# A fused linear-attention and feed-forward kernel: the sums of weights all on VectorE, and a new order, new banks and other zero products

## The chip, the cores and the metric

The kernel runs on one core of a Trainium2 chip. The metric is the device time of one execution in microseconds (us), as the median of several runs. A core has TensorE for matrix products (PE in the profile; PEld is its loading of weights), VectorE (DVE), ScalarE (ACT), GpSimd (POOL) and SyncE (SP), which here issues the DMA transfers. Each engine takes its instructions from a queue of its own, in order; an instruction that waits holds up all behind it on its engine.

## The reference

```
B, H, S, D = 4, 8, 768, 48          # attention; then 3072 tokens x 384
for t in range(S):
    cur = einsum('bhd,bhe->bhde', u[None] * k[:, :, t], v[:, :, t])
    y[:, :, t] = einsum('bhd,bhde->bhe', r[:, :, t], state + cur)
    state = w[:, :, t, :, None] * state + einsum('bhd,bhe->bhde', k[:, :, t], v[:, :, t])
x = y as (3072, 384)
h = x @ w_in                        # 384 -> 2048
g = where(h >= 1, h, where(h <= -1, 0, (h + 1) ** 2 / 4))
out = g @ w_out                     # 2048 -> 384
```

## The kernel before

The attention is cut into 12 units of 256 tokens, each into four chunks of 64, in which the recurrence is products of matrices: VectorE makes running products of the decays w (scans, L461 and L466) and scales r and k with them (L484); TensorE makes the products inside a chunk (L518), transposes (L588) and products with the state (L657, L622); VectorE keeps the part of the L518 products that belongs to earlier tokens (a predicated copy, L531).

The feed-forward part runs over 6 blocks of 512 tokens and 16 tiles of 128 ff columns. Every operand is split into a high and a low part, and a product is the sum of three. The 16 weight tiles are unpacked once: ScalarE L356 and L361, VectorE L375 and L378, ScalarE L352 for the high part, VectorE L382 for the low part. In blocks 0 to 2 a tile is a product with w_in (L1334, nine matmuls 128x512 into one PSUM bank), the gate on ScalarE and VectorE (L1113 to L1127) and a product with w_out (L1354, nine matmuls).

Blocks 3 to 5 use a scheme after Strassen for the product with w_out (`fast`). It works on pairs of ff tiles. The product with w_in is as before (L1334), then come ScalarE's Relu and Square (L939, L940) and VectorE's L941, which reads the bank for the last time and so frees it. VectorE makes differences of gates (L961, L963, L965), each is split by ScalarE (L946, L956) and VectorE (L947, L957), and TensorE accumulates terms of three matmuls 128x256 (L979) into six banks. That leaves two of the eight PSUM banks for the L1334 products.

The scheme also needs sums of weights, made once for each of the eight pairs by `sums_of`: two sums 128x256 and four or five 128x128 in one scratch area (`a` and `s`, parts of the tile p), ScalarE's copy of the high part (L915), and the low part, a subtraction 128x512. A pair can begin only when the pair before it is through with the scratch. Even pairs are computed by VectorE, odd ones by GpSimd; ScalarE's copies are the same for both.

Twelve loads of w through one buffer (`last`), each followed by ScalarE's L794 and L795, guard against decays for which the scheme of the chunks doesn't hold. The next of these loads can start only when ScalarE is through with the one before. They stand between ScalarE's steps for blocks 2 and 3.

A plan collects the 1,780 operations of all this, and three tables written out as numbers decide where they go: `ORDER` is the order in which they are emitted, and so the order of each engine's queue; `BANKS` gives each of 186 tenants of PSUM its bank; `FILLS` puts products with zeros (`zeros`, L307, results never read) ahead of given operations, which keep TensorE busy where it would stand still. Each entry of `FILLS` is (operation, bank, columns, added to what is there or not). The costs given to the plan's operations play no part in what is emitted.

Of the kernel before, what the change touches and what calls it, by code (L numbers as in the profile page):

```python
# [222 lines left out]
def attention_moe(tc, a):  # L223
# [667 lines left out]
    def sums_of(pair):  # L891
# [21 lines left out]
        for x, to in parts:  # L913
            n = to.stop - to.start
# [503 lines left out]
```

## Time and profile before

| what | us |
|---|---|
| median of three runs | 493.82 |
| the runs | 493.41 to 495.09 |
| the profiled execution | 493.96 |
| its span, first to last instruction | 492.4 |
| TensorE busy in it | 476.5 |
| VectorE busy | 405.9 |
| ScalarE busy | 308.4 |
| GpSimd busy | 27.9 |

The span is that of one profiled execution; what lies outside it is 1.56 us. A share of busy time is a mean over the whole span. The rows further down show single stretches of it: how long each engine was busy in a stretch, when an instruction started, how long it took, and behind it in brackets how long its engine had stood still and what ended that.

### The profile page before, as it was taken

Reading aid. Unit: us, or ns where it says so; the run is one execution under the profiler, and the core shown is the slowest. Engines: PE = TensorE matmul, PEld = TensorE weight load, DVE = VectorE, ACT = ScalarE, POOL = GpSimd, SP = SyncE. Lnnn points to the kernel's source line nnn. Section 1 sums busy time; section 2 is a strip of 40 time slices with the busy share of each in tenths; the row PEclk is TensorE's granted clock in tenths of the full one; section 3 lists DMA queues with packets and bytes.
Section 4 is the critical chain, followed back from the end, with each engine's and each line's share of the span. In section 5 each row is a group of like instructions: output and inputs, shape, how many; then the busy total and the mean of one; then the engine's idle time right before and its main releaser. Section 6 shows DMA issues by size and latency. Waiting matters only on the chain.

```text
span 492.4 us, 13209 instructions
## 1 busy us (share of the span) xinstructions
PE 476.5 (97%) x5629; PEld 414.9 (84%) x5629; DVE 405.9 (82%) x627; ACT 308.4 (63%) x581; POOL 27.9 (6%) x49
## 2 busy tenths in 40 slices
PE   6899999999999999999999998999999999999994
PEld 3679988889999988888888787887988998899894
DVE  5999999999998998998978875885868576784673
ACT  3869999736446564666535748887668365473660
POOL 4000000000000000000000331432000000000000
PEclk9999999999999999999999999999999999999999
DMA  8959923126460634634441013323110000010002
GB/s 306 368 189 398 379 85 110 62 74 203 139 208 4 229 94 139 208 125 137 125 147 48 29 31 87 64 54 76 23 64 2 0 1 1 29 37 0 1 3 70
DMA packets 35203, 53.50 MB, mean 109 GB/s; under 512 B 15744, under 2 KB 22592, under 8 KB 35136
## 3 DMA queue, kind: packets, MB, share of 16 engines
q1 hardware_dynamic: 34992, 52.45, 32.0%
q8 instruction: 46, 0.75, 0.6%
q14 instruction: 21, 0.17, 0.1%
q10 hardware_dynamic: 144, 0.13, 0.1%
HBM read 46.86 MB, written 4.72 MB: 105 GB/s over the span
## 4 chain that ended last, share of the span: by engine, by line
PE 83%; DMA 8%; ACT 4%; issue 2%; DVE 1%; SPq 1%; ACTq 0%
PE ps L1334 35%; PE ps L1354 19%; PE ps L979 15%; DMA last<-in_w 6%; PE ps L657 4%; PE ps L518 3%; PE ps L588 2%; PE ps L622 2%; PE ps L307 1%; ACT last L795 1%; ACT last L794 1%; PE ps L1218 1%; DMA wraw<-in_wbits 1%; DMA cst<-in_consts 1%; SPq L777 1%
## 5 line engine op out<-in xcount | busy, mean ns | idle before, releaser
L1334 PE MATMUL ps<-x,wt 128*128 128x512 f32 (+1 forms) x972 | 208.0, 366 | 2.0 <-DVE rk L941 1.6
L1334 PEld LDWEIGHTS ps<-x,wt 128*128 128x128 f32 x972 | 162.9, 188 | 30.2 <-DVE rk L941 2.4
L1354 PE MATMUL ps<-gh,wt 128*128 128x512 f32 (+1 forms) x360 | 75.3, 344 | 0.0
L941 DVE SCALAR_TENSOR_TENSOR rk<-rk,ps 128x512 f32<-128x512 f32 x48 | 32.9, 685 | 39.0 <-ACT rk L940 38.4
L1354 PEld LDWEIGHTS ps<-gh,wt 128*128 128x128 f32 x360 | 57.4, 188 | 7.7
L939 ACT ACTIVATE rk<-ps 128x512 f32<-128x512 f32 x48 | 28.5, 595 | 32.4 <-PE ps L1334 31.8
L1126 ACT CAST gh<-g 128x512 fp32r<-128x512 f32 (+1 forms) x47 | 28.6, 614 | 25.8 <-DVE g L1123 16.5
L1354 PE MATMUL ps<-gl,wt 128*128 128x512 f32 (+1 forms) x180 | 42.0, 342 | 0.0
L1113 ACT ACTIVATE g<-ps 128x512 f32<-128x512 f32 (+1 forms) x49 | 28.2, 584 | 15.1 <-PE ps L1334 11.9
L1123 DVE SCALAR_TENSOR_TENSOR g<-g,ps 128x512 f32<-128x512 f32 (+1 forms) x49 | 32.4, 671 | 1.5 <-ACT g L1114 1.4
L1354 PEld LDWEIGHTS ps<-gl,wt 128*128 128x128 f32 x180 | 30.0, 188 | 4.2
L1127 DVE TENSOR_TENSOR gl<-g,gh 128x512 fp32r<-128x512 f32 (+1 forms) x47 | 32.2, 691 | 1.6 <-ACT gh L1126 1.6
L461 DVE TENSOR_TENSOR_SCAN y<-wq,ends 128x520 f32<-128x520 f32 x24 | 29.6, 1233 | 3.9 <-POOL st L301 3.7
L940 ACT ACTIVATE rk<-rk 128x512 f32<-128x512 f32 x48 | 30.2, 631 | 1.0
L1114 ACT ACTIVATE g<-g 128x512 f32<-128x512 f32 (+1 forms) x49 | 29.7, 620 | 0.6
L466 DVE TENSOR_TENSOR_SCAN p<-wq,seeds 128x520 f32<-128x520 f32 x24 | 29.6, 1235 | 0.1
L947 DVE TENSOR_TENSOR g_again<-rk,nk_again 128x512 fp32r<-128x512 f32 x35 | 23.6, 686 | 6.2 <-ACT nk_again L946 6.2
L947 DVE TENSOR_TENSOR gl<-rk,gh 128x512 fp32r<-128x512 f32 x36 | 24.8, 690 | 4.5 <-ACT gh L946 3.5
L946 ACT CAST gh<-rk 128x512 fp32r<-128x512 f32 x36 | 22.0, 616 | 9.9 <-DVE rk L961 4.4
L946 ACT CAST nk_again<-rk 128x512 fp32r<-128x512 f32 x35 | 21.4, 615 | 6.9 <-DVE rk L965 3.6
L979 PE MATMUL ps<-nk_again,wt 128*128 128x256 f32 x130 | 24.8, 281 | 0.0
L898 POOL TENSOR_TENSOR p<-wt 128x256 f32<-128x256 f32 x8 | 7.6, 956 | 288.7 <-DVE p L898 288.7
(172 smaller groups left out, 865.9 us busy)
## 6 DMA issues: line engine op xcount, KB each, us to landing
rk<-in_rk SPq DMA_DIRECT2D x18, 512.0 KB, 4.0
wraw<-in_wbits SPq DMA_DIRECT2D x11, 768.0 KB, 8.0
nk<-in_nk SPq DMA_DIRECT2D x9, 768.0 KB, 5.6
wq<-in_w SPq DMA_DIRECT2D x24, 261.5 KB, 4.2
wraw<-in_wbits SPq DMA_DIRECT2D x15, 256.0 KB, 5.5
vn<-in_v SPq DMA_DIRECT2D x9, 384.0 KB, 3.9
rk<-in_rk SPq DMA_DIRECT2D x12, 256.0 KB, 6.6
last<-in_w SPq DMA_DIRECT2D x12, 256.0 KB, 3.0
```

The lines of the kernel that those rows point to most:

```text
L461: V.tensor_tensor_scan(out=y_[:, ::-1], data0=w[:, SEG:0:-1], data1=ends.rearrange("p n c -> p (n c)")[:, ::-1], initial=0.0, op0=ALU.mult ...
L466: V.tensor_tensor_scan(out=pv[:, q].rearrange("p n c -> p (n c)"), data0=w[:, 0:SEG], data1=sv, initial=0.0, op0=ALU.mult, op1=ALU.add)
L940: op("ACT", c, (), [qk], lambda: A.activation(gf, gf, AF.Square))
L941: op("DVE", 0.68, [("b", ht)], [qk], lambda: V.scalar_tensor_tensor(out=gf, in0=gf, scalar=1.0, in1=at(ht), op0=ALU.min, op1=ALU.max))
L946: op("ACT", 0.6, [key], fresh_in(("h", i, k)), lambda: A.copy(spare(k, i), x))
L947: op("DVE", 0.67, [key, ("h", i, k)], fresh_in(("l", i, k)), lambda: V.tensor_tensor(out=spare(k, 3 + i), in0=x, in1=spare(k, i).bitcast(F ...
L979: PE.matmul(at(sums_at[b][i])[:, half * UT : half * UT + UT], lhsT=w[wi], rhs=g[gi], start=(b, i) not in opened, stop=True, skip_group_che ...
L1114: op("ACT", c, (), [("g", gk)], lambda: A.activation(gs, gs, AF.Square))
L1123: op("DVE", 0.15 + 0.53 * k, [("b", ht)], [("g", gk)], lambda: V.scalar_tensor_tensor(out=gs, in0=gs, scalar=1.0, in1=hs(), op0=ALU.min, o ...
L1127: op("DVE", 0.145 + 0.54 * k, [("g", gk), ("gh", gk)], [("gl", gk)], lambda: V.tensor_tensor(out=gls, in0=gs, in1=ghs.bitcast(F32), op=ALU ...
L1334: nc.tensor.matmul(hp, lhsT=wx[f][:, cs], rhs=xt[:, j, :], start=first and n == 0, stop=n == 8, skip_group_check=not first)
L1354: nc.tensor.matmul(o[j], lhsT=wx[f][:, cs], rhs=gt, start=first and i == 0, stop=stop and i == 2, skip_group_check=True)
```

## The change

All of `sums_of` goes to VectorE. By the loops above, 30 operations of the odd pairs change engine: 8 of 128x256, 16 and one of 128x128, four of 128x512 and the last pair's low part of 128x128; ScalarE's copies stay. The number of operations is the same. All three tables are new. Of them the diff shows their first lines, and `FILLS` as a whole.

```diff
 ORDER = (
-    1, 14, 15, 2, 18, 0, 16, 4, 8, 11, 17, 7, 52, 19, 3, 27, 21, 22, 103, 115, 5, 10, 28, 62, 30, 20, 23, 64, 12, 29, 26, 31, 24,
+    0, 14, 15, 6, 1, 52, 16, 4, 2, 17, 22, 18, 103, 19, 27, 21, 62, 28, 26, 115, 30, 31, 29, 33, 32, 46, 23, 42, 35, 8, 20, 40, 47,
...
 BANKS = (
-    6, 5, 6, 5, 7, 0, 4, 7, 6, 7, 5, 6, 1, 0, 4, 7, 5, 0, 2, 7, 4, 5, 1, 2, 0, 7, 6, 1, 5, 6, 2, 4, 4, 0, 0, 3, 5, 6, 0, 1, 3, 7, 2,
+    1, 5, 5, 6, 7, 0, 7, 4, 5, 7, 6, 5, 1, 0, 6, 7, 4, 5, 4, 2, 1, 0, 7, 7, 6, 2, 5, 0, 1, 0, 6, 6, 2, 0, 3, 3, 6, 5, 1, 1, 3, 7, 2,
...
 FILLS = (
-    (46, 6, 512, False), (46, 6, 64, False), (40, 5, 512, False), (45, 2, 512, False), (45, 2, 64, False), (57, 7, 256, False),
-    (86, 7, 512, False), (86, 7, 64, False),
+    (46, 5, 512, False), (46, 5, 512, False), (55, 2, 256, False),
 )
...
     def sums_of(pair):
         f = 2 * pair
-        on, e = ("POOL", G) if pair % 2 else ("DVE", V)
-        cost = (lambda n: 0.25 + 0.0024 * n) if pair % 2 else (lambda n: 0.13 + 0.00105 * n)
+        on, e = "DVE", V
+        cost = lambda n: 0.13 + 0.00105 * n
```

The tables of the changed kernel take one line less, so that its lines bear numbers lower by one: L1334 is L1333 there. What the new tables do is seen at three places.

TensorE's queue at the beginning of the program, before. L690 and L314 clear banks, L307 are zero products; L518 are the products inside a chunk, L588 transposes, L657 and L753 later steps of the first unit.

```order
L690 LDWEIGHTS zero_75
L690 MATMUL ps_110<-zero_75 128x512
L307 MATMUL ps_110<-zero_75 128x512
L307 MATMUL ps_110<-zero_75 128x64
L588 MATMUL ps_110<-cst_67,xf_109 128x128 x4
L307 MATMUL ps_110<-zero_75 128x512
L518 MATMUL ps_110<-rk_83,nk_85 64x64 x16
L518 MATMUL ps_110<-xf_108,xf_109 64x64 x16
L518 MATMUL ps_110<-rk_82,nk_85 64x64 x16
L588 MATMUL ps_110<-cst_67,xf_108 128x128 x4
L307 MATMUL ps_110<-zero_75 128x512
L307 MATMUL ps_110<-zero_75 128x64
```

And after:

```order
L689 MATMUL ps_110<-zero_75 128x512
L306 MATMUL ps_110<-zero_75 128x512 x2
L587 MATMUL ps_110<-cst_67,xf_109 128x128 x4
L517 MATMUL ps_110<-rk_83,nk_85 64x64 x16
L517 MATMUL ps_110<-rk_82,nk_85 64x64 x16
L517 MATMUL ps_110<-xf_108,xf_109 64x64 x16
L587 MATMUL ps_110<-cst_67,xf_108 128x128 x4
L313 MATMUL ps_110<-zero_75 64x128 x2
L656 MATMUL ps_110<-r_90,vn_86 48x64 x16
L517 MATMUL ps_110<-xf_108 64x64 x16
L752 MATMUL ps_110<-ob_106,nk_85 128x128 x6
L306 MATMUL ps_110<-zero_75 128x256
```

The zero products now stand in two places, ahead of the first transpose and behind the fourth L517 group, with none among the L517 groups; before, there were two more places, one of them ahead of the first of these groups and one ahead of the fourth.

TensorE's queue where block 2 ends and block 3 begins, before: the first products with w_in of block 3 (L1334), the last products with w_out of block 2 (L1354) and the first terms of the scheme (L979).

```order
L979 MATMUL ps_110<-kt_again,wt_345 128x256 x6
L1334 MATMUL ps_110<-x_95,wt_513 128x512 x9
L1334 MATMUL ps_110<-x_95,wt_627 128x512 x9
L1354 MATMUL ps_110<-gh_101,wt_1236 128x512 x6
L1354 MATMUL ps_110<-gl_104,wt_1236 128x512 x3
L979 MATMUL ps_110<-kt_again,wt_513 128x256 x6
L1334 MATMUL ps_110<-x_95,wt_616 128x512 x9
L1354 MATMUL ps_110<-gh_102,wt_1239 128x512 x6
L1354 MATMUL ps_110<-gl_105,wt_1239 128x512 x3
L1354 MATMUL ps_110<-gh_100,wt_1444 128x512 x6
L1354 MATMUL ps_110<-gl_103,wt_1444 128x512 x3
L1334 MATMUL ps_110<-x_95,wt_770 128x512 x9
```

And after:

```order
L1333 MATMUL ps_110<-x_95,wt_495 128x512 x9
L1333 MATMUL ps_110<-x_95,wt_612 128x512 x9
L1353 MATMUL ps_110<-gh_101,wt_1228 128x512 x6
L1353 MATMUL ps_110<-gl_104,wt_1228 128x512 x3
L1333 MATMUL ps_110<-x_95,wt_621 128x512 x9
L1353 MATMUL ps_110<-gh_102,wt_1234 128x512 x6
L1353 MATMUL ps_110<-gl_105,wt_1234 128x512 x3
L1353 MATMUL ps_110<-gh_100,wt_1439 128x512 x6
L1353 MATMUL ps_110<-gl_103,wt_1439 128x512 x3
L1333 MATMUL ps_110<-x_95,wt_759 128x512 x9
L1333 MATMUL ps_110<-x_95,wt_842 128x512 x9
L978 MATMUL ps_110<-kt_again,wt_459 128x256 x6
```

Five products with w_in of block 3 now stand ahead of the first accumulation of the scheme in this piece, where before two accumulations stood among four of them.

ScalarE's queue at the ninth and tenth of the twelve guards (L794, L795), before; L915 is the copy of a sum of weights, L939 and L940 are Relu and Square, L946 and L956 copies for the split.

```order
L794 ACTIVATE last_96<-last_96 128x512
L795 ACTIVATE last_96,above_78<-last_96,minus_one_72 128x512
L946 CAST nk_again<-rk_83 128x512
L915 CAST st_again<-p_87 128x512
L939 ACTIVATE rk_82<-ps_110 128x512
L794 ACTIVATE last_96<-last_96 128x512
L940 ACTIVATE rk_82<-rk_82 128x512
L946 CAST nk_again<-rk_84 128x512
L795 ACTIVATE last_96,above_78<-last_96,minus_one_72 128x512
```

And after:

```order
L793 ACTIVATE last_96<-last_96 128x512
L794 ACTIVATE last_96,above_78<-last_96,minus_one_72 128x512
L945 CAST nk_again<-rk_84 128x512
L938 ACTIVATE rk_83<-ps_110 128x512
L945 CAST gh_101<-rk_84 128x512
L939 ACTIVATE rk_83<-rk_83 128x512
L938 ACTIVATE rk_83<-ps_110 128x512
L914 CAST vn_again<-p_87 128x512
L945 CAST gh_102<-rk_84 128x512
L939 ACTIVATE rk_83<-rk_83 128x512
L945 CAST gh_100<-rk_82 128x512
L793 ACTIVATE last_96<-last_96 128x512
```

Between the ninth guard's last step and the tenth guard's first stood three instructions; now there are nine, and none of the guard's stands between a Relu and its Square.

## Rows read from the trace of the kernel before

**Rows 1.** The page: busy time by engine; TensorE's busy tenths in 40 slices.

```profile
PE 476.5 (97%) x5629; PEld 414.9 (84%) x5629; DVE 405.9 (82%) x627; ACT 308.4 (63%) x581; POOL 27.9 (6%) x49
PE   6899999999999999999999998999999999999994
```

**Rows 2.** Windows: stretch, us, busy PE, PEld, DVE, ACT, POOL; clock, DMA share, GB/s.

```profile
0.00:16.00 16.00, 10.39 (x176) 6.18 (x180) 9.81 (x15) 6.84 (x13) 5.62 (x19) 1.00 0.89 330
16.00:42.00 26.00, 24.98 (x541) 20.84 (x531) 25.89 (x35) 20.21 (x37) 0.00 (x0) 1.00 0.78 281
42.00:285.00 243.00, 243.00 (x3694) 211.03 (x3693) 228.64 (x322) 154.99 (x295) 5.03 (x7) 1.00 0.42 141
285.00:345.00 60.00, 57.02 (x334) 49.25 (x334) 42.63 (x76) 45.45 (x91) 17.29 (x23) 1.00 0.27 64
345.00:486.00 141.00, 140.97 (x906) 127.62 (x905) 98.48 (x182) 80.93 (x148) 0.00 (x0) 1.00 0.05 16
```

**Rows 3.** Timeline, TensorE, first 17 us: start, duration, engine, line, operation [idle before].

```profile
5.74 2.39 PE L307 MATMUL ps<-zero 128*128 128x512 f32 x4 [1.91 <-ACT look L318]
7.92 1.06 PE L588 MATMUL ps<-cst,xf 128*128 128x128 f32 x4
8.78 1.50 PE L307 MATMUL ps<-zero 128*128 128x512 f32 x2
11.19 0.65 PE L518 MATMUL ps<-rk,nk 64*64 64x64 f32 x32
11.77 0.66 PE L588 MATMUL ps<-cst,xf 128*128 128x128 f32 x4
13.96 1.29 PE L307 MATMUL ps<-zero 128*128 128x512 f32 x4 [1.53 <-DVE r L531]
15.18 0.69 PE L518 MATMUL ps<-xf 64*64 64x64 f32 x32
```

**Rows 4.** Timeline, VectorE, 8 to 17 us.

```profile
11.96 0.73 DVE L531 COPY_PREDICATED r<-cst,ps 128x512 f32<-128x512 int32 x1 [1.48 <-issue]
15.94 0.73 DVE L531 COPY_PREDICATED r<-below,ps 128x512 f32<-128x512 int32 x1 [0.95 <-PE ps L518]
```

**Rows 5.** Timeline, TensorE, 298 to 343 us: the three longest stalls.

```profile
299.19 2.33 PE L1334 MATMUL ps<-x,wt 128*128 128x512 f32 x9 [0.44 <-DVE rk L941]
302.33 0.50 PE L979 MATMUL ps<-gh,wt 128*128 128x256 f32 x2 [0.80 <-ACT gh L946]
340.66 2.36 PE L1334 MATMUL ps<-x,wt 128*128 128x512 f32 x9 [1.14 <-DVE rk L941]
```

**Rows 6.** Waits of the whole span (us in total, times, longest), then ScalarE's timeline.

```profile
ACT last L794 <- DMA last<-in_w: 13.1, 11, 3.4
338.74 0.63 ACT L794 ACTIVATE last<-last 128x512 f32<-128x512 f32 x1 [1.35 <-DMA last<-in_w]
339.28 0.61 ACT L940 ACTIVATE rk<-rk 128x512 f32<-128x512 f32 x1
```

**Rows 7.** Groups by line and form, 270 to 345 us, GpSimd then VectorE: busy, mean ns.

```profile
L898 POOL TENSOR_TENSOR p<-p 128x128 f32<-128x128 f32 x17 | 9.1, 556 | 5.2 <-DVE r_again L898 2.1 <-DVE fl_again L898 1.3 <-DVE vn_again L898 0.7
L898 DVE TENSOR_TENSOR p<-p 128x128 f32<-128x128 f32 x16 | 5.0, 329 | 0.1
L898 DVE TENSOR_TENSOR p<-wt 128x256 f32<-128x256 f32 x8 | 3.2, 416 | 0.0
L898 DVE TENSOR_TENSOR r_again<-p,fl_again 128x512 fp32r<-128x512 f32 x1 | 0.7, 683 | 0.0
L961 DVE TENSOR_TENSOR rk<-rk 128x512 f32<-128x512 f32 x7 | 5.9, 846 | 2.5 <-PE ps L657 2.4
```

**Rows 8.** Timeline, VectorE, 299 to 331 us: forms alone, and beside GpSimd.

```profile
299.17 0.69 DVE L961 TENSOR_TENSOR rk<-rk 128x512 f32<-128x512 f32 x1
317.83 1.68 DVE L961 TENSOR_TENSOR rk<-rk 128x512 f32<-128x512 f32 x1
329.30 1.22 DVE L898 TENSOR_TENSOR vn_again<-p,vn_again 128x512 fp32r<-128x512 f32 x1
```

158 rows, old and new, of tables (BANKS, ORDER) are left out of this document.

## The prediction

> **What bounds the kernel now.** I read the page's busy times first, then the windows, then the timelines of the stretches in which TensorE stands still. TensorE is busy 476.5 of 492.4 us [rows 1], so at most 16 us can be had without taking away products, and the windows say where they lie [rows 2]: from 42 to 285 us TensorE is busy 243.00 of 243.00, from 345 to 486 us 140.97 of 141.00. Nothing that the new order does inside these two stretches can help; it can only do harm. What is left is the start (0 to 42 us), the change-over from block 2 to block 3 (285 to 345 us, TensorE idle 60.00 - 57.02 = 2.98 us) and the last 6 us behind TensorE's end, where the order is nearly as before.
>
> The two stretches have different limits. **At the start VectorE sets the end**: from 16 to 42 us it is busy 25.89 of 26.00 us [rows 2], and TensorE, full of small products and zeros, becomes dense only when VectorE has got through the first units and the first weight tiles. So a microsecond that VectorE wins before 16 us comes out at the end. It stands still twice there, 1.48 and 0.95 us [rows 4]. The first of the two copies starts at 11.96, and the L518 group that it follows ended at 11.19 + 0.65 = 11.84; this group stands in TensorE's queue behind a zero product of 1.50 us that began at 8.78 [rows 3]. The second waits for the L518 group at 15.18, which stands behind zero products that began at 13.96, and these themselves had waited 1.53 us for VectorE [rows 3]. Both waits are made by zero products standing where VectorE waits for what comes behind them.
>
> **In the change-over ScalarE's queue sets it.** TensorE's three longest stalls are 0.44, 0.80 and 1.14 us [rows 5]. Two of the three wait for VectorE's L941, which frees one of the two banks, and L941 waits for ScalarE's Square. At 338.74 ScalarE waited 1.35 us for a guard's load that stood in its queue between a Relu and its Square (339.28); L941 and TensorE at 340.66 followed [rows 5, 6]. Over the span ScalarE waits 13.1 us in eleven pieces for these loads [rows 6].
>
> **The change, part by part.**
>
> Zero products. Before, 16 instructions and 2,496 columns, now 6 and 1,280. Two pieces, 512 and 64 columns, are four instructions and took 1.29 us at 13.96 [rows 3]. TensorE's time for them costs nothing by itself, since it stood still there anyway; what counts is who waits. In the new queue no zeros stand among the first L517 groups, so the 1.48 and 0.95 us, together 2.43, lose their cause. Not all of it arrives at 42 us: two loads (the constants and the first weight tile) change places in SP's queue, and GpSimd's clearing of the destination of the first copies stands behind one more small copy. By walking through the new order with the durations of before, VectorE finds its next wait later, for an L517 group of the second unit that needs ScalarE's copy first; I put that at 0.9 us, as the 0.95 of the wait that it resembles most [rows 4]. Taken: 2.43 - 0.9 = 1.5 us gained. The bounds: 2.5 gained (all of it), and nothing gained.
>
> The clock belongs to this part. The first four zeros took 2.39 us where the same forms took 1.29 later, and the first transposes 1.06 against 0.66 [rows 3], while the window shows a granted clock of 1.00, the level of 2.4 GHz [rows 2]: TensorE's opening is slow in its first 8 us. In the new order the first L517 groups come after fewer products. If they run at the early pace, three groups of 0.65 and two of transposes of 0.66 take some 1.7 times as long, 3 x 0.65 x 0.7 + 2 x 0.66 x 0.6 = 2.2 us more, which would eat the gain. I take the full pace, since the new opening still has its clearing and two zeros of 512 columns in front, and no wait for ScalarE (1.91 us before [rows 3]); the other end goes to a rival.
>
> The sums. Onto VectorE come 8 of 128x256 at 0.416, 17 of 128x128 at 0.329, four of 128x512 at 0.683 and one small one at about 0.33 [rows 7]: 3.3 + 5.6 + 2.7 + 0.3 = 12.0 us. GpSimd took 0.556 for its 128x128 [rows 7], and 5.03 + 17.29 = 22.3 us in all [rows 2]. VectorE gets back what GpSimd had stretched: L961 takes 0.69 alone but 1.68 at 317.83 [rows 8], its mean of seven is 0.846 [rows 7], so 7 x 0.156 = 1.1, and the 128x512 low part 1.22 for 0.68 [rows 7, 8], together 1.6. Net +10.4, of which the share 17.29 / 22.3 falls into 285 to 345 us: +8.1. VectorE is busy 42.63 of 60 there [rows 2], so 50.7, and there is room. Beside work that hides it, this costs nothing; if it lands in front of an L941 that TensorE waits for, it costs up to its own length. The page "SBUF — State Buffer" of the Trainium skill (section "Who interferes with whom") says that a VectorE instruction with two SBUF inputs contends with a GpSimd instruction that reads SBUF. The 1.68 us of rows 8 agrees; by that rule all of the 22.3 us could have cost VectorE something, and the gain would be larger than the 1.6 that the rows carry.
>
> The change-over itself. The new order brings five products with w_in ahead of the first accumulation of the scheme, so that ScalarE and VectorE start on more gates while TensorE still has products of block 2; and the guards stand farther apart (nine instructions between the ninth and tenth instead of three), no longer between a Relu and its Square there. Walking through it with the durations of before, I find about two thirds of the stalls left, the longest one again a product that waits for L941 to free a bank, now late because of VectorE's own queue. So 2.98 becomes about 2.0: 1.0 us gained. The bounds: 3.0 gained (no stall left), and on the other side the added 8.1 us, of which a part comes out (below).
>
> New banks. In the dense stretch an attention product now takes a bank that ScalarE empties only just before. The trace of before has no such wait there; the nearest rows are TensorE's waits for a bank to be freed, 0.44 and 1.14 us [rows 5]. I take one of 0.4; between nothing and 1.1.
>
> The sum: -1.5 - 1.0 + 0.4 = -2.1 us. The profiled execution took 493.96 (its span of 492.4 and 1.56 around it), so 491.9; it lies 0.14 above the median of 493.82, which leaves **491.7** for a median.
>
> **The rivals.** About 0.3%, 1.5 us, is what a measurement of this kernel can tell from no change.
>
> *All of both goes.* The zeros were the whole cause at the start, and the wider guards the whole cause later: -2.43 - 2.98 = -5.4, so 488.4. For it: each wait named is at a place that the new order rewrites. Against it: my walk finds a next wait in both stages.
>
> *The start gives nothing.* The first products run at the early pace (2.2 us against 2.4 gained), or the constants' later place holds up VectorE; and the change-over swaps one wait for another: about 493.8, within 492.4 to 495.2. For it: the slow opening is in the rows, and TensorE loses 1,216 columns of zeros that kept it busy. Against it: the opening has one wait less.
>
> *VectorE becomes the bound of the change-over: slower.* The sums stand in its one queue, and L941, on which both banks hang, stands behind them. Of the 8.1 us, if half comes out as TensorE's idle time: -1.5 + 0.4 + 4.1 = +3.0, so 496.8. It decides from the point at which a third, 2.6 us, comes out (-1.5 + 0.4 + 2.6 = +1.5). For it: two of the three stalls wait for L941 already [rows 5]. Against it: VectorE has 17.4 us idle in the stage [rows 2], and one engine that does all sums no longer hands the scratch to another. "Perfetto Trace Analysis" of the Trainium skill (section "Optimizing Scalar/DVE Operations") says that moving work from a saturated VectorE to another engine, GpSimd even, may make sense, though a shared read port may spoil it; here the change goes the other way, and by that rule this case is the one to expect. With 42.63 of 60 us VectorE isn't saturated in this stage, so the trace bears it out only in part.
>
> **How the numbers follow.** The forecast, 490.5 to 492.4, has 0.45; all of both 0.12; the start that gives nothing 0.28; slower 0.15. Faster by over 0.3% (below 492.3): 0.45 + 0.12 = 0.57; within: 0.28; slower (above 495.3): 0.15. The range leaves out half of the best case (0.06) and most of the slower one (0.12): from 488.6, the bounds -2.5 and -2.7 together, to 495.2, the upper end of the case without a gain.
>
> **What will show it.** VectorE's L530 copies (L531 before) should start earlier than 11.96 and 15.94 with no wait above 0.9 us ahead of them, and TensorE should become dense at about 40 instead of 42 us. From 285 to 345 us TensorE should be idle about 2 us instead of 2.98, L960 (L961 before) should take 0.69 throughout, and ScalarE should wait less than 13.1 us for the guards' loads. The prediction is wrong at the start if the first L517 groups take over 1 us each; in the change-over if TensorE's waits name L940 (L941 before) with more than 3 us in sum, or if VectorE is busy over 55 of the 60 us. A stall of over 1 us between 42 and 285 us would say that the new banks cost more than I took.

## The result, and the profile after

| what | before | after |
|---|---|---|
| median, us | 493.86 (4 runs, 493.41 to 495.09) | 485.55 (4 runs, 484.79 to 487.18) |
| ratio of the runs | | 0.983, 95% interval 0.980 to 0.986 |
| profiled execution, us | 493.96 | 484.79 |
| its span, us | 492.4 | 483.2 |
| TensorE busy, us | 476.5 | 472.3 |
| VectorE busy, us | 405.9 | 407.0 |
| GpSimd busy, us | 27.9 | 4.5 |

The changed kernel is 8.3 us faster, 1.7%. The forecast was 491.7, its best case 488.4. The sign was right, the size not. The profiled execution is the fastest of the four, so its span shows 9.2 us and not 8.3.

First the windows of the changed kernel: stretch, us, busy time of PE, PEld, DVE, ACT and POOL with the number of instructions, granted clock, DMA share, GB/s.

```profile
0.00:16.00 16.00, 11.69 (x191) 7.93 (x192) 11.55 (x17) 8.18 (x15) 4.47 (x19) 0.89 0.88 310
16.00:42.00 26.00, 24.36 (x519) 20.52 (x519) 25.72 (x35) 20.96 (x39) 0.00 (x0) 1.00 0.88 326
42.00:285.00 243.00, 242.59 (x3686) 210.90 (x3685) 228.09 (x323) 152.32 (x294) 0.00 (x0) 1.00 0.41 137
285.00:345.00 60.00, 59.59 (x353) 52.66 (x352) 49.37 (x109) 49.15 (x98) 0.00 (x0) 1.00 0.28 64
```

Against [rows 2] the change-over is the stretch that changed most: TensorE idle 0.41 us instead of 2.98, with VectorE at 49.37 of 60 us.

To see where the 9.2 us of span went, I laid the starts of all matmuls of both traces side by side by the product work done (each matmul counted with the usual spacing of its form, zero products left out), and read the changed kernel's lead at the same work. "Start" is the lead where the kernel before stands at 64 us, "middle" what it gains up to 295 us, "change-over" up to 355 us, "later" up to 481 us, and "end" by how much the time from the start of TensorE's last matmul to the end of the span became shorter. The table has one profiled execution of each kernel run in this study, each against the same execution of the kernel before; minus is a loss. The runs e1 to i2 are told one by one further down.

| kernel | start | middle | change-over | later | end | median of its runs, us |
|---|---|---|---|---|---|---|
| changed kernel | 1.7 | 0.4 | 4.7 | 0.2 | 2.1 | 485.55 |
| e1: changed, sums on GpSimd | 0.8 | 0.4 | 4.5 | 0.2 | 2.2 | 485.69 |
| e2: before, sums on VectorE | -1.4 | 0.0 | 0.3 | -0.1 | 0.7 | 493.49 |
| e3: before, fewer zeros | 1.8 | -0.8 | -2.1 | 0.0 | 0.4 | 494.68 |
| e4: before, last two stores | -1.0 | 0.0 | 0.5 | 0.0 | 0.1 | 494.12 |
| f1: before, last 21 operations | -0.7 | -1.2 | 0.1 | 0.0 | 2.0 | 492.61 |
| f2: before, guards spread by products | -0.2 | 0.0 | -2.9 | -0.8 | 1.8 | 497.35 |
| f3: changed, guards tight by products | -1.4 | 0.4 | -10.7 | 0.4 | 2.2 | 501.46 |
| f4: three edits, guards as in f2 | 1.5 | -0.6 | -1.6 | -0.8 | 2.1 | 493.19 |
| h1: before, guards even | -0.2 | -0.4 | 4.3 | -1.8 | 0.5 | 491.43 |
| h2: changed, guards close | 1.5 | 0.4 | -7.1 | 0.4 | 1.9 | 496.53 |
| h3: before, three edits, guards even | 1.7 | -1.3 | 4.3 | -1.7 | 1.9 | 489.38 |
| i1: h3 with the guards earlier | 1.9 | -0.8 | -0.6 | 0.1 | 2.0 | 490.20 |
| i2: changed, guards even | 1.5 | 0.4 | 4.3 | -0.3 | 2.0 | 486.04 |

In e2, e4, f1, f2 and h1 the opening up to 42 us is that of the kernel before, instruction for instruction; their "start" lies between -1.4 and -0.2. So a start moves by some 1.4 us from one execution to the next with nothing changed in it, and a difference of that size between two single starts proves nothing by itself. The opening of the changed kernel stands in five rows, too: 1.7, 0.8, -1.4 (f3), 1.5 and 1.5. Taken together, the five mean 0.8 and the six executions of the old opening -0.6, a gain of about 1.4 us.

The scatter of the starts goes with TensorE's granted clock. Its records in the trace begin, with 1.00, at 9.7 us in the kernel before and at 10.0, 10.1, 11.0, 11.5 and 12.0 us in f2, h1, f1, e4 and e2: the later they begin, the smaller the lead. The four kernels without the zeros among the first groups go the same way: 9.3, 9.4, 10.4 and 11.2 us in i1, e3, h3 and f4, with leads of 1.9, 1.8, 1.7 and 1.5. In e1 and f3 the records show 0.50 for longer than in the changed kernel: until 14.8 and 14.5 instead of 12.2 us, and in f3 once more from 21.3 to 24.7 us.

The change-over repeats to half a microsecond where nothing was changed in it, but for e3, and the end to 0.7, but for f2; both are taken up below.

The medians of the kernel before in the four sets of runs were 493.25, 493.08, 494.05 and 492.96; the verdicts below compare with that of the same set.

**Start.** Timeline of the changed kernel, TensorE, then VectorE's first copy behind the L517 products.

```profile
2.07 3.51 PE L306 MATMUL ps<-zero 128*128 128x512 f32 x4
8.37 0.74 PE L587 MATMUL ps<-cst,xf 128*128 128x128 f32 x4 [2.79 <-DVE y L460]
9.04 1.99 PE L517 MATMUL ps<-rk,nk 64*64 64x64 f32 x64
11.15 1.35 DVE L530 COPY_PREDICATED r<-cst,ps 128x512 f32<-128x512 int32 x2 [0.51 <-POOL vn L294]
```

VectorE's first wait is 0.51 instead of 1.48 us, and the view names GpSimd's clearing of the copy's destination for it; the second, of 0.95 us [rows 4], is gone.

**Change-over.** TensorE's longest wait there, and ScalarE's for the guards' loads (us in total, times, longest).

```profile
328.08 1.65 PE L1333 MATMUL ps<-x,wt 128*128 128x512 f32 x6 [0.41 <-DVE rk L940]
ACT last L793 <- DMA last<-in_w: 5.3, 5, 1.6
```

13.1 us of waiting in eleven pieces [rows 6] have become 5.3 in five; three TensorE waits of 0.44, 0.80 and 1.14 [rows 5] have become one of 0.41.

**End.** SyncE's issues of the last stores: start, time until the last issue of the group is through, count. Three of the kernel before, then two of the changed one.

```profile
484.77 2.44 SPq L1071 DMA_DIRECT2D out_y<-xf  x3
```

```profile
477.03 0.42 SPq L1070 DMA_DIRECT2D out_y<-xf  x1
477.74 0.33 SPq L1070 DMA_DIRECT2D out_y<-xf  x1
```

Before, the second of the three issues, at 485.19, takes 1.49 us and holds up the two behind it; ScalarE issues a store as well, at 484.77. The span ends 6.5 us after TensorE's last matmul starts. After, no issue takes over 0.42 us, and it is 4.4 us.

The waiting for the issue is the smaller part of these 2.1 us. The last store is issued 1.45 us after the start of the last matmul before, and 1.15 us after it in the changed kernel. The rest is its landing, the last number of each line (before, then after):

```profile
out_y<-xf SPq DMA_DIRECT2D x1, 128.0 KB, 4.1
out_y<-xf SPq DMA_DIRECT2D x1, 128.0 KB, 2.3
```

### The profile page after: what moved, and what is told of

Its sections match the earlier page's. It is cut to its first block, busy times and chain, and to the rows that moved or that the text cites. A ratio compares the mean times of both kernels' runs of the same rounds, so it can differ in the third digit from the quotient of the medians.

```text
span 483.2 us, 13174 instructions
## 1 busy us (share of the span) xinstructions
PE 472.3 (98%) x5619; PEld 414.2 (86%) x5619; DVE 407.0 (84%) x657; ACT 304.1 (63%) x581; POOL 4.5 (1%) x19
## 4 chain that ended last, share of the span: by engine, by line
PE 82%; DMA 7%; ACT 5%; DVE 3%; issue 1%; SPq 1%; ACTq 0%; DVEq 0%
PE ps L1333 35%; PE ps L1353 19%; PE ps L978 16%; PE ps L656 4%; PE ps L517 3%; PE ps L587 2%; DMA rk<-in_rk 2%; DMA last<-in_w 2%; PE ps L621 2%; DMA wraw<-in_wbits 2%; ACT last L794 1%; DMA wq<-in_w 1%; ACT last L793 1%; ACT gh L945 1%; DVE y L460 1%
## 5 line engine op out<-in xcount | busy, mean ns | idle before, releaser
L1333 PE MATMUL ps<-x,wt 128*128 128x512 f32 (+1 forms) x972 | 207.6, 366 | 0.5 <-DVE rk L940 0.4
L1333 PEld LDWEIGHTS ps<-x,wt 128*128 128x128 f32 x972 | 163.4, 188 | 28.9 <-DVE rk L940 0.8
L940 DVE SCALAR_TENSOR_TENSOR rk<-rk,ps 128x512 f32<-128x512 f32 x48 | 32.4, 684 | 27.9 <-ACT rk L939 27.8
L946 DVE TENSOR_TENSOR g_again<-rk,nk_again 128x512 fp32r<-128x512 f32 x35 | 23.8, 686 | 10.2 <-ACT nk_again L945 10.0
L939 ACT ACTIVATE rk<-rk 128x512 f32<-128x512 f32 x48 | 29.8, 629 | 0.6
L946 DVE TENSOR_TENSOR gl<-rk,gh 128x512 fp32r<-128x512 f32 x36 | 24.5, 686 | 5.8 <-ACT gh L945 5.7
L945 ACT CAST nk_again<-rk 128x512 fp32r<-128x512 f32 x35 | 21.3, 616 | 7.8 <-DVE gl L946 2.5
L978 PE MATMUL ps<-gh,wt 128*128 128x256 f32 x120 | 23.2, 280 | 0.0
```

The source lines that it names most:

```text
L939: op("ACT", c, (), [qk], lambda: A.activation(gf, gf, AF.Square))
L940: op("DVE", 0.68, [("b", ht)], [qk], lambda: V.scalar_tensor_tensor(out=gf, in0=gf, scalar=1.0, in1=at(ht), op0=ALU.min, op1=ALU.max))
L945: op("ACT", 0.6, [key], fresh_in(("h", i, k)), lambda: A.copy(spare(k, i), x))
L946: op("DVE", 0.67, [key, ("h", i, k)], fresh_in(("l", i, k)), lambda: V.tensor_tensor(out=spare(k, 3 + i), in0=x, in1=spare(k, i).bitcast(F ...
L978: PE.matmul(at(sums_at[b][i])[:, half * UT : half * UT + UT], lhsT=w[wi], rhs=g[gi], start=(b, i) not in opened, stop=True, skip_group_che ...
L1333: nc.tensor.matmul(hp, lhsT=wx[f][:, cs], rhs=xt[:, j, :], start=first and n == 0, stop=n == 8, skip_group_check=not first)
```

## Whose gain is it: the engine or the order?

The edit of e1 is one line of the changed kernel, that of e2 the same line the other way round in the kernel before.

```diff
-        on, e = "DVE", V
+        on, e = ("POOL", G) if pair % 2 else ("DVE", V)
```

> The new order, banks and zero products, with the sums of the odd pairs back on GpSimd. Theory 'order' (the 4.5 us won between 285 and 345 us come from the new order: guards farther apart, products ahead of the first accumulation): at most 1 us slower than the changed kernel, about 486.5, TensorE without a stall over 1 us from 285 to 345. Theory 'engine' (the gain comes from the sums' leaving GpSimd): the 4.5 us are lost again, about 490, and L961's form is stretched to over 0.8 us in the mean.

Measured: 485.69 (ratio to before 0.983, 0.979 to 0.987), as fast as the changed kernel.

> The kernel before with all sums on VectorE and nothing else changed. Theory 'order': 493.9, or slower by up to 4 us, since VectorE gets 10 us more work in a queue that was not laid out for it; the waits for the guards' loads stay at about 13 us. Theory 'engine': about 489.4.

Measured: 493.49 (ratio 0.999, 0.997 to 1.001), no difference. The theory "engine" falls at both ends: the move of 30 operations, which the change is named for, is worth nothing that can be measured, and all of the gain is the tables' (`ORDER`, `BANKS`, `FILLS`; no run takes `BANKS` by itself). The window of e1 says why nothing is lost:

```profile
285.00:345.00 60.00, 59.54 (x351) 52.59 (x350) 46.89 (x86) 49.00 (x99) 16.77 (x21) 1.00 0.26 60
```

GpSimd works 16.77 us in the same stretch, and TensorE is busy all the same. In e2 VectorE's busy time is 409.2 against 405.9 of the whole span: 30 operations more cost it 3.3 us, not the 10.4 that I worked out.

## The start: the zero products

e3 leaves three entries out of the table of the kernel before.

```diff
-    (46, 6, 512, False), (46, 6, 64, False), (40, 5, 512, False), (45, 2, 512, False), (45, 2, 64, False), (57, 7, 256, False),
-    (86, 7, 512, False), (86, 7, 64, False),
+    (46, 6, 512, False), (46, 6, 64, False), (57, 7, 256, False), (86, 7, 512, False), (86, 7, 64, False),
```

> The kernel before without the three zero products that stand among the first L518 groups (512 columns; 512 and 64 columns). Theory 'zeros' (they made VectorE's two waits of 1.48 and 0.95 us): both waits go or fall below 0.5 us, TensorE gets dense some 1.5 us earlier, about 492.4. Rival 'loads' (the start was won by the new order of the loads and of the other instructions): 493.9, the waits stay or come back at the next copy.

Measured: 494.68 (ratio 1.002, 0.999 to 1.004). VectorE's timeline in e3 shows the mechanism that was expected:

```profile
10.88 0.72 DVE L530 COPY_PREDICATED r<-cst,ps 128x512 f32<-128x512 int32 x1 [0.31 <-issue]
13.98 0.71 DVE L530 COPY_PREDICATED r<-below,ps 128x512 f32<-128x512 int32 x1
```

1.48 has become 0.31, 0.95 nothing, and TensorE leads by 1.8 us at 64 us; e3, f4, h3 and i1, the four kernels without these zeros, lead by 1.5 to 1.9, the five with the old opening by none. So the zeros made the two waits. But the lead didn't reach the end, and that was not expected. It went in two places. At 252 us VectorE waits for a load of r and k:

```profile
252.59 0.69 DVE L483 TENSOR_TENSOR rk<-rk,y 128x512 f32<-128x512 f32 x1 [2.61 <-DMA rk<-in_rk]
341.65 1.65 PE L1333 MATMUL ps<-x,wt 128*128 128x512 f32 x6 [1.80 <-DVE rk L940]
```

The kernel before starts the same instruction at 253.28, behind a wait of 1.53 us for the same load. That is 0.7 us later and not 1.8: TensorE's and VectorE's lead is lost there to a transfer. How long this load takes varies, though. In f1, whose order is that of the kernel before up to there, VectorE starts it only at 255.22:

```profile
255.22 0.69 DVE L485 TENSOR_TENSOR rk<-rk,y 128x512 f32<-128x512 f32 x1 [2.80 <-DMA rk<-in_rk]
```

The two loads of r and k around that time take, in their median, 4.7 to 4.9 us from issue to landing in the kernel before, e2, e4 and f2, 5.7 in h1, 6.2 in f1, and 5.8 to 6.6 in e3, f4, h3 and i1, which come to it early. So it isn't shown that the lead as such is lost there. And in the change-over (second row) TensorE waits 1.80 us where it waited 1.14 [rows 5], since the guards' loads didn't come earlier by as much as ScalarE did: its first wait for them grew from 3.4 to 4.1 us. A microsecond won ahead of a chain that has its own pace, as these loads have, can be lost in it.

## The end: the last stores

e4 only exchanges the last two stores; f1 puts the last 21 operations in the order of the changed kernel.

```diff
# e4, the end of ORDER
-    1764, 1765, 1778, 1773, 1779,
+    1764, 1765, 1773, 1779, 1778,
# f1, the end of ORDER; 1771 is VectorE's sum for the fourth store, 1777 that store
-    1770, 1757, 1758, 1776, 1759, 1760, 1769, 1761, 1762, 1771, 1775, 1763, 1772, 1774, 1777, 1764, 1765, 1778, 1773, 1779,
+    1771, 1757, 1770, 1758, 1759, 1776, 1760, 1769, 1777, 1761, 1762, 1775, 1763, 1772, 1774, 1764, 1765, 1773, 1779, 1778,
```

> The kernel before with its last two stores as in the changed kernel (both behind VectorE's last sum). From TensorE's last matmul to the end it was 6.4 us before and 4.3 us after. Theory 'stores': 4.3 us here too, about 491.7. Rival 'chance' (a store took long in one profiled execution): 6.4 us, or anything between, and 493.9 in the median.

Measured: 494.12 (ratio 1.002, 0.999 to 1.004), and 6.5 us from TensorE's last matmul to the end, as before. That the stores' exchange made the difference was wrong, and so was "chance": the 6.5 stood again.

> The kernel before with its last 21 operations in the order of the changed kernel: VectorE's sum that feeds the fourth store comes earlier, so that its store leaves 1 us earlier. Theory 'pile': before, three stores are issued within 0.5 us and the third issue holds SP's queue for 1.3 to 1.5 us; with the new order it is 4.4 us from TensorE's last matmul to the end instead of 5.9 to 6.5, about 491.5. Rival 'other cause' (the transfers land sooner for a reason further up): 5.9 to 6.5 us, 493.5.

Measured: 492.61 (ratio 0.998, 0.996 to 1.000), and 4.5 us to the end instead of 6.5. f1's second and third issue on SyncE:

```profile
485.80 1.04 SPq L1072 DMA_DIRECT2D out_y<-xf  x2
```

With the fourth store's sum made ahead of two others, its store leaves 1 us earlier, the long issue doesn't occur, and the last store lands 2.3 us after its issue, as in the changed kernel. All nine kernels with the new last operations end 4.3 to 4.7 us after the last matmul; of the six with the old ones five end after 5.9 to 6.5, and one, f2, after 4.7 with an issue of 1.1 us. In these five the last store takes 3.5 to 4.1 us to land, in f2 2.6, in the nine 2.2 to 2.6. So the late landing goes with the three stores issued together; why it lands late no run shows. The median of f1 isn't clear of the noise: its runs scatter by 2 us and those of the kernel before by 5, and its profiled execution lost 1.2 us again in the middle, 0.9 of it at the load of r and k above.

## The change-over: the guards

f2 and f3 move only the 36 operations of the twelve guards, f2 in the kernel before to the places of the changed kernel, f3 the other way round, both counted from the products with w_in of block 3.

> The kernel before with the twelve guards (load, Abs, Relu) where the changed kernel has them, counted from the products with w_in of block 3; all else as before. Theory 'guards' (ScalarE's queue stands on loads that can't come faster than one in 4.4 us): TensorE's stalls from 285 to 345 us fall from about 4 us to 1, the wait for the loads from 13 to about 6 us; 490. Rival 'products' (it is the new order of TensorE's products and banks): the stalls stay or move, about 493.5.

Measured: 497.35 (ratio 1.008, 1.005 to 1.011), slower.

> The changed kernel with the twelve guards as close together as in the kernel before, counted from the same products; all else as in the changed kernel. Theory 'guards': ScalarE waits over 12 us for the loads, TensorE stands still 3 us or more between 285 and 345 us; 488.5 to 490. Rival 'products': 485.6, the new order of the products takes the waits up.

Measured: 501.46 (ratio 1.014, 1.010 to 1.018), far slower. Neither theory had this. ScalarE and TensorE in f2 (lines one higher than before):

```profile
327.74 0.63 ACT L795 ACTIVATE last<-last 128x512 f32<-128x512 f32 x1 [2.68 <-DMA last<-in_w]
333.01 0.63 ACT L795 ACTIVATE last<-last 128x512 f32<-128x512 f32 x1 [2.27 <-DMA last<-in_w]
334.02 0.61 ACT L947 CAST gh<-rk 128x512 fp32r<-128x512 f32 x1
334.68 0.58 PE L980 MATMUL ps<-gh,fl_again 128*128 128x256 f32 x1 [3.91 <-ACT gh L947]
```

Up to there f2 had won 3.4 us in the change-over; then two guards stand 5 us apart, ScalarE waits for their loads, and TensorE stands still for 3.91 us for the split behind the second. Counting from products had put some of the twelve too close, since the two kernels' products stand in other orders. f3 failed likewise, with one wait of TensorE of 9.8 us. The cause that both theories disputed shows itself all the more, but neither run tells it apart from the order of the products. f4 put f2's guards together with the edits of e3 and the end.

> The kernel before with three edits together: the zero products among the first L518 groups left out, the guards spread as in the changed kernel, the last 21 operations as there. The sums stay on GpSimd for odd pairs, and the order and banks of all else stay as before. If these three places carry the gain: -2 (start), -3.5 (change-over), -2 (end), about 486. If the new order of the products or the banks is needed too: 488 to 491.

Measured: 493.19 (ratio 0.999, 0.997 to 1.001): 1.5 at the start and 2.1 at the end won, and lost again in the change-over by the same stall.

So the places were set anew, by TensorE's work: in h1 one guard for each 6 us in the kernel before, in h2 the old, close places in the changed kernel.

> The kernel before with the twelve guards set evenly, one for each 6 us of TensorE's work, and each load issued right behind the guard before it; all else as before. The earlier spreading put three of them 4 us apart and ran into a wait of 4.1 us. Theory 'guards': no wait of ScalarE for the loads over 1 us, TensorE's stalls from 285 to 345 us below 1 us in sum; about 490. Rival 'products' (the new order of products and banks is needed): TensorE still stands 2 us or more there; 492 to 493.5.

Measured: 491.43 (ratio 0.995, 0.992 to 0.997), faster.

> The changed kernel with its guards at the places of the kernel before, counted in TensorE's work (the first ten about 4 us apart); all else as in the changed kernel. Theory 'guards': ScalarE waits over 12 us for the loads in sum and TensorE stands 3 us or more; 488.5 to 491. Rival 'products': 485.6 to 486.5.

Measured: 496.53 (ratio 1.007, 1.004 to 1.009): 11 us slower than the changed kernel. The windows of h1, which has no wait of ScalarE for these loads at all any more, and the waits of h2:

```profile
285.00:345.00 60.00, 59.75 (x387) 53.04 (x379) 46.33 (x86) 45.91 (x90) 18.67 (x23) 1.00 0.21 51
345.00:400.00 55.00, 53.92 (x341) 48.35 (x340) 37.14 (x66) 34.91 (x66) 0.00 (x0) 1.00 0.14 35
```

```profile
ACT last L794 <- DMA last<-in_w: 19.1, 11, 3.3
PE ps L1334 <- DVE rk L941: 3.5, 4, 1.1
```

With nothing moved but the guards, the kernel before wins 4.3 us in the change-over, nearly the changed kernel's 4.7: TensorE is busy 59.75 of 60 us with the old order of products, old banks, and sums on GpSimd. And the changed kernel with close guards falls 7.1 us behind the kernel before in that stretch, 11.8 behind its own 4.7. Not all of that is waiting: behind two groups of stalls the granted clock is 0.50, from 303.5 to 306.8 and from 320.5 to 323.8 us. The theory "guards" holds, and the five products ahead of the first accumulation are not needed for it.

But h1 gives 1.8 back between 345 and 400 us. ScalarE (L940 Relu, L941 Square, L795 and L796 the guard, in h1's numbers) and TensorE there:

```profile
362.00 0.58 ACT L940 ACTIVATE rk<-ps 128x512 f32<-128x512 f32 x1
362.48 0.62 ACT L795 ACTIVATE last<-last 128x512 f32<-128x512 f32 x1
363.13 0.72 ACT L796 ACTIVATE last<-last,minus_one 128x512 f32<-128x512 f32 x1
363.85 0.61 ACT L941 ACTIVATE rk<-rk 128x512 f32<-128x512 f32 x1
365.24 2.12 PE L1335 MATMUL ps<-x,wt 128*128 128x512 f32 x8 [0.55 <-DVE rk L942]
```

It is the picture of 338.74 [rows 5, 6] without the wait for the load: a guard's 1.37 us between a Relu and its Square, in a stretch in which the bank that the Square's follower frees is the next that TensorE needs. In the changed kernel the last two guards stand at 355 and 375 us without such a stall.

h3 is h1 with the edits of e3 and f1; i1 is h3 with a guard for each 5.5 us, the first 6 us earlier; i2 is the changed kernel with even guards.

> The kernel before without the zero products among the first L518 groups, with the guards set evenly as in the run before, and with the last 21 operations of the changed kernel. If the three places carry the gain: -2 (start), -3.5 (change-over), -2 (end) from 493.1, so about 486. If products and banks are needed too: 488 to 491.

Measured: 489.38 (ratio 0.993, 0.990 to 0.995). Three local edits win 4.7 of the 8.3 us. What is missing stands mostly in two columns of the table: 1.7 in the middle (of h3's loss there 1.3 is at the load of r and k, as in e3) and 1.9 behind the change-over.

> As the run with three edits and even guards, but one guard for each 5.5 us of TensorE's work, from 6 us earlier on, so that the last stands about 10 us earlier. That run lost 1.7 us again between 360 and 380 us, in two stalls beside the last two guards. Theory 'guards' (any place of a guard beside a stretch where ScalarE is short costs): those stalls go, nothing new comes between 285 and 345 us; 487.5 to 488. Rival 'products' (before's order of products has those stalls in store whatever stands there): they stay, or a new one comes; 489.4.

Measured: 490.20 (ratio 0.995, 0.993 to 0.997). The stalls of 360 to 380 us are gone (0.1 instead of -1.7), as expected of "guards", but the change-over loses 0.6 where h3 won 4.3. The first guard is the one:

```profile
294.62 0.63 ACT L794 ACTIVATE last<-last 128x512 f32<-128x512 f32 x1 [3.33 <-DMA last<-in_w]
299.17 0.63 ACT L794 ACTIVATE last<-last 128x512 f32<-128x512 f32 x1 [1.43 <-DMA last<-in_w]
301.69 0.51 PE L979 MATMUL ps<-gh,wt 128*128 128x256 f32 x2 [1.33 <-ACT gh L946]
```

Its load isn't there yet, and the split that TensorE waits for stands behind the first two guards; behind that stall the granted clock is 0.50, from 302.9 to 306.1 us, which makes the loss larger. In h1 and h3 the first guard comes at about 300 us and waits for nothing.

> The changed kernel with its guards set evenly, one for each 6.4 us of TensorE's work; all else as in the changed kernel. There ScalarE still waited some 5 us for the loads of the guards, and one stall of TensorE of 0.57 us was left. Theory 'guards': no such wait, the stall goes, 485.0. If the guards of the changed kernel were well enough placed: 485.6, no difference that can be measured. If its order of products has no room for other places: slower, 486 or more.

Measured: 486.04 (ratio to before 0.986, 0.982 to 0.989), no better than the changed kernel: the waits for the loads fall to 2.5 us, and two stalls of TensorE of 0.5 to 0.6 us at 345 and 360 us take the place of the one that goes. No kernel of this study beats the changed one.

## Why the prediction was right or wrong

**The bound** was read rightly: the gain lies at the start, in the change-over and behind TensorE's end, and the dense stretches gave 0.4 and 0.2 us. The first mistake was to put nothing into the sum for the last 6 us "behind TensorE's end, where the order is nearly as before": I had only compared orders there. VectorE's sum for the fourth store was among the operations that moved, and the trace of before shows the long issue and the late landing when the last stores are read one by one. This term was 0 in the sum and measured -2.1.

**The start**, -1.5, measured -1.7 in the profiled execution, and e3 shows the mechanism named. That the size comes so near is partly luck: the same opening gave between -1.4 and 1.7 in five executions, and e3 shows that such a lead can be lost again at 253 and 300 us, which the prediction didn't ask. The rival's "early pace" came true in part and didn't decide: after 2.79 us of standing TensorE's first two L517 groups took 1.99 instead of 2 x 0.65 us. The 1.00 that the prediction took from [rows 2] for the opening is no reading ahead of 9.7 us, where the records of the clock begin.

**The change-over**, -1.0, measured -4.7; here lies most of the error, in two steps. First, I took 2.98 us as all that could be won, which is TensorE's idle time in the window. Matmuls' ends are modelled, so a short standstill hides in them: the spacing between starts, over the usual one, gives 0.61 + 0.97 + 0.38 + 0.53 + 1.30 = 3.8 us for the five longest stalls alone. Second, I walked through the new order and let two thirds of the stalls stand. The new order left one of 0.41 us. The walk made VectorE's queue the next bound; it had room, as the windows said. The named cause, guards standing in ScalarE's queue between steps that TensorE waits for, was right, and h1 shows that moving them is enough.

**The new banks**, +0.4, show no cost: the middle gained 0.4. What they do by themselves no run tells.

**The sums** at nothing: right (e1, e2), with a wrong size below it. VectorE's busy time grew by 3.3 us in e2, not 10.4. Three things make the difference. The sums' own durations (L898) grew by 10.0 us, not 12.0. Other forms gave back 4.1 and not 1.6: in the changed kernel L960 takes 0.684 in the mean of eight instead of 0.846 [rows 7], and L962 0.419 instead of 0.694. And durations overlap in the trace: all of VectorE's add up to 6.3 us more, of which only 3.3 are busy time. The Trainium skill ("SBUF — State Buffer", section "Who interferes with whom") says that a VectorE instruction with two SBUF inputs contends with a GpSimd instruction that reads SBUF; these means agree. The 1.6 us that I let it have was too little.

**The rivals.** "All of both goes" was the nearest, and it too had 488.4, without the end and with 2.98 for the change-over. "VectorE becomes the bound" had its mechanism: in f2, f3, h2 and i1 waits for L941 or for splits behind a full queue do cost several us, but the queue is ScalarE's. The Trainium skill ("Perfetto Trace Analysis", section "Optimizing Scalar/DVE Operations") speaks of moving work away from a saturated VectorE; that condition wasn't met here: with all sums on it VectorE is at 49.37 of 60 us.

## What to carry to other kernels

A load into a single buffer that is used again and again has a pace of its own (here 4.4 us at least from one guard to the next). By these runs each use belongs in an in-order queue no closer than that pace, not before its load can be there (i1), and not between two steps of a chain that frees what the bounding engine needs next (h1 at 362 us). Size what a stage can win from the spacing of starts, not from idle time in a window, and look at the last stores one by one. When a change comes as an edit with a name and new tables, run the edit alone: here it was worth nothing, and the tables 8 us.

## What the runs showed of the hardware

TensorE's granted clock fell to half behind some of its standstills. In f2 it stood for 3.91 us; the windows of that place, and then those of the changed kernel's opening, where it stood for 2.79 us up to 8.37:

```profile
330.00:334.50 4.50, 0.77 (x7) 0.56 (x5) 0.69 (x1) 2.20 (x5) 0.00 (x0) 0.97 0.44 117
334.50:337.00 2.50, 2.32 (x8) 2.00 (x9) 1.46 (x3) 1.67 (x5) 0.00 (x0) 0.50 0.21 44
337.00:340.00 3.00, 3.00 (x9) 2.32 (x8) 1.28 (x3) 0.15 (x1) 0.00 (x0) 0.50 0.27 57
```

```profile
8.00:10.00 2.00, 1.63 (x40) 1.38 (x44) 2.00 (x5) 1.68 (x5) 1.62 (x5) 0.69 0.98 384
10.00:12.00 2.00, 2.00 (x73) 1.88 (x66) 1.49 (x3) 0.91 (x1) 0.98 (x5) 0.50 1.09 427
```

0.50 is the level of 1.2 GHz, 1.00 that of 2.4. So a stall of 4 us can cost more than 4: f2's change-over loses 2.9 although up to the stall it had won over 3.

The length of one standstill doesn't tell whether the clock falls. Behind one of 1.70 us in h2 and one of 1.33 us in i1 it fell (first and second row), and behind one of 1.80 us in e3 it stayed at 1.00 (third row), as behind the one of 1.53 us in the kernel before [rows 3]:

```profile
303.50:306.80 3.30, 3.30 (x16) 3.20 (x15) 1.00 (x4) 1.92 (x5) 0.00 (x0) 0.50 0.45 163
302.90:306.10 3.20, 3.20 (x17) 3.20 (x16) 2.86 (x8) 2.20 (x6) 0.00 (x0) 0.50 0.51 180
339.00:345.00 6.00, 4.20 (x23) 3.35 (x22) 3.63 (x7) 4.00 (x9) 0.46 (x1) 1.00 0.22 44
```

In the first microseconds a clock of 1.00 in a window can mean that nothing is recorded there: the trace's records begin at 9.7 us in the kernel before and at 13.3 us in h2. In h2 the first two L518 groups, ahead of 13.3 us, take 1.99 us, as long as the same two at a recorded 0.50 in e1; in the kernel before a group behind 9.7 us takes 0.65.

The issue of one store of 128 KB took 1.1 to 1.5 us on SyncE in each of the six executions in which three of these last stores were issued within half a microsecond, two on SyncE and one on ScalarE; of the other issues of these stores most took 0.3 to 0.4 us, the longest 0.95. Why the load of r and k takes between 4.7 and 6.6 us stays open; no run took its transfer apart.
